# Attention with a filled-in feed-forward: half of a split filling product moved behind the third pair of scores

## The chip, the cores and the metric

The kernel runs on one core of a Trainium2 chip. The metric is the device time of one execution in microseconds (us), given as the median of several executions. The times of single instructions come from one profiled execution.

## The reference, cut to what matters

The input x has 2048 rows of 512. It is normalised row by row and goes two ways. The one is attention with 32 heads of width 16 over all 2048 rows; the other is a dense layer with a squared ReLU (width 1792), whose result gates the attention.

```
xn = layernorm(x)
q, k, v = heads(xn @ wqkv)                      # 32 heads of 16
s = softmax(q @ k.T * 0.25) @ v @ wo            # 2048 x 2048 scores a head
h = relu(xn @ w1 + b1); g = silu(h * h @ w2 + b2)
out = x + s * g
```

## The kernel before, in words

All data is float32. Projections and scores are done with a number split in a high and a low part, so that one product becomes three (high by high, high by low, low by high).

**Stages.** A first stage normalises x and makes keys, queries and values. Then comes the main loop (line 777) of 128 turns, which does the attention and, beside it, the dense layer and at the end the output projection. A short tail follows.

**Steps and turns.** A step is four heads (qd), 512 queries (qc) and 128 keys (kb); a turn handles four steps. For each step TensorE makes the scores of four heads as two pairs: `scores(i, p)` (line 291) issues two matmuls of 64 rows by 512 columns into the two banks of one PSUM tile S. The first of a pair uses rows 0 to 63 of the array ("half 0"), the second rows 64 to 127 ("half 1"), so the two can run side by side. ScalarE then takes the exponential of the whole tile (`exps`, line 284, recorded as L286). There are two S tiles in the loop, used in turn: a pair of scores must wait until the exponential of the pair two before it has read its tile. Three of four steps of a turn go that way: the turn's first and second pair (step i + 1), the third and fourth (i + 2), and the fifth and sixth (i + 4, which belongs to the next turn's values).

**Single scores.** The fourth step (i + 3) goes another way, `aside` (line 300): a single matmul into the one bank `lin`, which VectorE copies to SBUF (L305) before the next single score may use the bank. There are four in a turn, on half 0, half 1, half 0, half 1; their exponentials read the copies.

**Filling products.** The dense layer and the output projection are cut into blocks of half-height products, 64 rows by 512 columns, that accumulate in the two banks of the tile `spare`. `lin(h)` (line 357) issues the next one for half h (recorded as L330), `lin(0, 1)` one for each half. An ordinary turn issues up to twelve for each half. A list `fill` says which block belongs to which turn. In ordinary turns one product of half 1 is divided into two of 256 columns each, `lin_part(1, 0)` and `lin_part(1, 1)` (line 363, recorded as L350), so that, with the single score of half 1 between them, half 1 has as many columns as half 0. In a few turns (`make and end`) a block begins and ends in one turn; these have no divided product and are ordered otherwise.

**Values.** At the end of a turn `values` (line 555) multiplies the exponentials of four steps by the values, with all 128 rows of the array and 32 columns at a time, into the bank `acc` (L561): 16 matmuls, each recorded twice.

**What sets the order.** The program is written with a manual schedule: each engine executes its instructions in the order in which the code issues them. A wait for another engine stands on an instruction (for a matmul, on its weight load), and what is behind it on that engine comes after it. Loads and stores for later blocks are hung in by due times (`at`, `happen`) and go through the queues of SyncE and GpSimd; VectorE also evicts `spare` and splits weights, mostly while the values are multiplied.

The part of a turn around the change, lines 787 to 808:

```
for _ in range(3):
    lin(0, 1)
lin(0)
...
    lin_part(1, 0)
    aside(i + 3, 0, 1)
    lin(0)
    lin_part(1, 1)
exps(i + 2, 0, scores(i + 2, 0))
...
    lin(0, 1)
    lin(0, 1)
exps(i + 2, 1, scores(i + 2, 1))
```

Of the kernel before, what the change touches and what calls it, by code (L numbers as in the profile page):

```python
# [46 lines left out]
@with_exitstack  # L47
def mha_ffn_kernel(ctx: ExitStack, tc: tile.TileContext, x, wqkv, wo, bx, w1, b1, w2, b2, out):
    nc = tc.nc
    x, out = x[0], out[0]  # L50
    ctx.enter_context(tc.manual_schedule())
    keep = ctx.enter_context(tc.tile_pool(name="keep", bufs=1))
    dram = ctx.enter_context(tc.tile_pool(name="dram", bufs=1, space=DRAM))

    ident = keep.tile([128, 128], FT, name="ident")
    make_identity(nc, ident)
    vt = keep.tile([128, NK, VW], FT, name="vt")
    nvalid = keep.tile([1, 1], I32, name="nvalid")
    stat = keep.tile([128, 80], FT, name="stat")

    kdram = [[dram.tile([128, 2, 1024], FT, name=f"kd{g}_{h}") for h in range(2)] for g in range(4)]
    qdram = [[dram.tile([128, 2, 512], FT, name=f"qd{g}_{c}") for c in range(NC)] for g in range(4)]
    xdram = [dram.tile([128, 2, 4, 512], FT, name=f"xd{c}") for c in range(3)]

    udram = [[dram.tile([2, 2, 16, 4, 512], FT, name=f"ud{g}_{c}") for c in range(NC)] for g in range(4)]
    zdram = [[dram.tile([4, 512], FT, name=f"zd{q}_{c}") for c in range(NC)] for q in range(NQ)]
    gdram = dram.tile([S, D], FT, name="gd")

    with tc.tile_pool(name="sb", bufs=1) as sb, tc.tile_pool(name="ps", bufs=1, space=PSUM) as ps:
        fast_path(tc, sb, ps, locals())  # L70
    general_path(tc, dram, nvalid, ident, vt, kdram, qdram, gdram, x, wo, out)


def fast_path(tc, sb, ps, env):
# [11 lines left out]
    def t(shape, dt, tag):  # L86

        cnt[0] += 1
        p = ps if tag in ("S", "lin", "acc") else sb
        if tag in BUFS:  # L90
            turn[tag] = turn.get(tag, -1) + 1
            n = turn[tag] % BUFS[tag]
            tag = f"{tag}{places[n] if tag == 'S' else n}"
        return p.tile(shape, dt, tag=tag, name=f"{tag}_{cnt[0]}")
# [189 lines left out]
    def exps(i, p, src):  # L284
        if src is not None:
            act.activation(ptile[i, p], src, AF.Exp, scale=SCALE)  # L286
# [4 lines left out]
    def scores(i, p):  # L291

        if i < len(steps):
            sc = t([128, 2, 512], FT, "S")
            place(i, p)
            for hp in range(2):
                score(i, p, hp, sc[:, hp])
            return sc

    def aside(i, p, hp):  # L300

        if hp == 0:
            place(i, p)
        score(i, p, hp, single)
        dve.tensor_copy(ptile[i, p][:, hp], single)  # L305
# [51 lines left out]
    def lin(*halves):  # L357
        if pair[0]:
            for half in halves:
                j = half ^ swapped[0]  # L360
                pair[0][j].issue(half, lin_banks[j])

    def lin_part(half, part):
        if pair[0]:
            j = half ^ swapped[0]
            pair[0][j].issue_part(half, lin_banks[j], part)

    def swap():
        if pair[0]:
            while any([pair[0][half ^ swapped[0]].issue(half, lin_banks[half ^ swapped[0]]) for half in range(2)]):  # L370
                pass
            swapped[0] ^= 1
            if not swapped[0]:
                pair[0][0].evict()
                pair[0] = None
# [21 lines left out]
    def split_piece(eng=None):  # L397
        if at_piece[1] == len(pieces):
            return
        j, layer, m = pieces[at_piece[1]]  # L400
        at_piece[1] += 1
        raw, q = raws.pop(0), PAIRS[m][1]
        wf[layer, m] = [t([128, 4, 256] if layer == 1 else [128, 2, 512], FR, f"wf{layer}{p}{q}") for p in "hl"]
        split(*wf[layer, m], raw, eng or dve, pool)
        load_piece()
# [149 lines left out]
    def values(i):  # L555
        qd, qc, kb = steps[i]
        if kb == 0:
            acc[0] = t([128, 512], FT, "acc")
        for j in (1, 2, 3, 0) if i % 2 else (0, 1, 2, 3):
            o = (4 * qd + j) * 17  # L560
            mm(acc[0][32 * j:32 * j + 32], vt[:, kb, o:o + 32], ptile[i, j // 2][:, j % 2],  # L561
               start=kb == 0, stop=kb == NK - 1)

    def finish(i):

        qd, qc, kb = steps[i]
        if kb < NK - 1:
            return
        if i == len(steps) - 1:
            return  # L570
        ou = t([128, 512], FT, "ou")
        cast(act if turn_ends_first[0] else dve, ou, acc[0])
        sp.dma_start(zdram[qd][qc], ou[16::32])
        for j in range(4):
            sp.dma_start(udram[qd // 2][qc][0, qd % 2, :, j], ou[32 * j:32 * j + 16])
        n = i // 4
        events.setdefault(2 * n + 2, []).insert(0, (load_sums, (qd, qc)))
        at(n + 2, rowsums, qd, qc)
# [174 lines left out]
    def happen(time):  # L753
        for fn, a in events.pop(int(2 * time), ()):
            fn(*a)
# [10 lines left out]
    def rest(i, dst):  # L766

        group(dst, lambda p: onorm[2, 3][p][:, cut[i]], lambda p: wos[0][p][:, 3])

    def end_rest(i, src):  # L770

        o = t([128, 512], FT, f"wf2{'hl'[i // 2]}{i % 2}")
        dve.scalar_tensor_tensor(o, src, 0.5, gsb[2, i // 2][:, i % 2], op0=OP.mult, op1=OP.mult)
        pool.dma_start(out[1024 + 128 * i:1152 + 128 * i], o, accum_op=OP.add)

    turn_ends_first = [False]
    for n in range(TURNS):
        i = 4 * n
        happen(n)
        make, end, split_now = fill[n]  # L780
        if make:
            pair[0] = make()
        exps(i + 1, 0, scores(i + 1, 0))
        aside(i + 3, 0, 0)
        lin(1)
        exps(i + 1, 1, scores(i + 1, 1))
# [3 lines that stand above are left out]
        if make and end:  # L790
            lin(1)
            lin(0)
            aside(i + 3, 0, 1)
        else:

            lin_part(1, 0)
            aside(i + 3, 0, 1)
            lin(0)
            lin_part(1, 1)
        exps(i + 2, 0, scores(i + 2, 0))  # L800
        if make and end:
            for j in range(2):
                pair[0][j].issue_whole(lin_banks[j])
            swap()
        else:
            lin(0, 1)
            lin(0, 1)
        exps(i + 2, 1, scores(i + 2, 1))
        aside(i + 3, 1, 0)
        lin(1)  # L810
        exps(i + 3, 0, ptile[i + 3, 0])
        lin(0, 1)
        lin(0, 1)
        last = [scores(i + 4, 0)]
# [3 lines that stand above are left out]
        aside(i + 3, 1, 1)  # L818
        exps(i + 3, 1, ptile[i + 3, 1])
        last.append(scores(i + 4, 1))  # L820
        for p in range(2):
            exps(i + 4, p, last[p])
        if n == TURNS - 1:
            two = t([128, 2, 512], FT, "S")
            rest(0, two[:, 0])
        turn_ends_first[0] = n < LAST and end and fill[n][0] is None and fill[n - 1][2] and n % per in (7, 15, 23)
        swap()
        if n == LAST - 1:
            gsb.update({(2, i): y[2, i] for i in range(2)})
        if n == TURNS - 1:  # L830
            end_rest(0, two[:, 0])
        happen(n + 0.5)
        if split_now:
            split_piece()
        for j in range(4):
            values(i + j)
        finish(i + 3)
# [169 lines left out]
```

## Time and profile before

| | |
|---|---|
| median of 3 runs | 1267.33 us (1266.63 to 1267.73) |
| profiled execution | 1266.77 us |
| its span | 1265.00 us |
| granted TensorE clock, mean | 0.999 |
| exponentials of score tiles (L286, P<-S) | 768, mean 1020 ns |
| exponentials of copied scores (L286, P<-P) | 256, mean 1060 ns |
| copies of single scores (L305) | 512, mean 691 ns |
| value matmuls (L561), records | 4096, mean 595 ns |
| pairs of scores (L282, S), matmuls | 1536, mean 423 ns |

The span runs from the first to the last recorded instruction; the execution's own time is 1.77 us longer. PE is TensorE's matmuls, PEld its weight loads, DVE VectorE, ACT ScalarE, POOL GpSimd and SP SyncE. A row such as "S<-QA,KA 64*128 64x512" names the tile that is written and those that are read: 64 rows by 128 columns of weights, 64 by 512 of data. Matmuls are pipelined and their recorded ends are modelled: records of one half overlap, so that the time from start to start tells more than the length. "[0.21 <-ACT P L286]" behind a row is idle time of that engine ahead of it and what ended it.

### The profile page before, as it was taken

How to read it: one execution, taken by the hardware profiler on the slowest of the kernel's cores; microseconds unless marked ns; L12 is line 12 of the kernel's file. 1: busy time of each engine (PE TensorE's matmuls, PEld its weight loads, DVE VectorE, ACT ScalarE, POOL GpSimd, SP SyncE). 2: the span in 40 equal slices, each digit the busy share in tenths (PEclk: the TensorE clock that was granted, in tenths of full speed). 3: DMA queues.
4: the chain of work that ended last, by engine and by line, in shares of the span. 5: the costliest groups of instructions: out<-in, count | busy, mean ns of one | idle time of the engine just before them, and what ended most of it. 6: DMA issues, size and time to landing. Idle time of an engine off the chain costs nothing.

```text
span 1265.0 us, 24997 instructions
## 1 busy us (share of the span) xinstructions
PE 1252.7 (99%) x10029; PEld 715.2 (57%) x10029; DVE 677.8 (54%) x1064; ACT 1041.3 (82%) x1123; POOL 258.9 (20%) x150
## 2 busy tenths in 40 slices
PE   9999999999999999999999999999999999999997
PEld 7888755555555555555555555555555555545554
DVE  5542255455555654545465555555554545566655
ACT  4222588989899899999998999999889989999884
POOL 5000122122211221312023221220331212322112
PEclk9999999999999999999999999999999999999999
DMA  7565513232233132121423222333223122463445
GB/s 265 209 233 195 217 44 105 59 94 52 84 126 110 60 102 66 42 91 46 153 76 109 57 80 60 93 126 101 60 65 88 48 88 60 143 217 116 145 135 121
DMA packets 84940, 137.32 MB, mean 109 GB/s; under 512 B 26058, under 2 KB 40408, under 8 KB 83284
## 3 DMA queue, kind: packets, MB, share of 16 engines
q1 hardware_dynamic: 81668, 126.25, 30.7%
q0 software_dynamic: 2720, 8.65, 2.5%
q8 instruction: 79, 1.29, 0.4%
q10 hardware_dynamic: 432, 0.79, 0.2%
q14 instruction: 41, 0.34, 0.1%
HBM read 94.24 MB, written 41.41 MB: 107 GB/s over the span
## 4 chain that ended last, share of the span: by engine, by line
PE 96%; DVE 2%; ACT 1%; issue 1%; POOL 1%; DMA 0%; DVEq 0%; ACTq 0%
PE acc L561 36%; PE spare L330 24%; PE S L282 17%; PE S L111 9%; PE lin L282 8%; PE spare L350 1%; PE S L204 1%; ACT P L286 0%; PE spare L339 0%; POOL hl L104 0%; DMA P<-in_A_x_dram 0%; DVE P L305 0%; PE acc L111 0%; DVE st L166 0%; ACT wf2h L98 0%
## 5 line engine op out<-in xcount | busy, mean ns | idle before, releaser
L286 ACT ACTIVATE P<-S 128x1024 f32<-128x1024 f32 x768 | 739.6, 1020 | 68.1 <-PE S L282 64.9
L305 DVE COPY P<-lin 128x512 f32<-128x512 f32 x512 | 353.9, 691 | 463.0 <-PE lin L282 429.7
L561 PE MATMUL acc<-P,vt 128*32 128x512 f32 x4096 | 466.0, 595 | 0.0
L282 PE MATMUL S<-QA,KA 64*128 64x512 f32 x1536 | 344.3, 423 | 0.3
L286 ACT ACTIVATE P<-P 128x1024 f32<-128x1024 f32 x256 | 271.2, 1060 | 31.8 <-DVE P L305 31.3
L561 PEld LDWEIGHTS acc<-P,vt 128*32 128x32 f32 x4096 | 120.1, 109 | 263.8 <-issue 263.8
L282 PEld LDWEIGHTS S<-QA,KA 64*128 64x128 f32 x1536 | 163.9, 183 | 177.0 <-ACT P L286 141.1
L282 PE MATMUL lin<-QA,KA 64*128 64x512 f32 x512 | 213.8, 418 | 0.6 <-DVE P L305 0.3
L104 POOL TENSOR_TENSOR wf1l<-wr,wf1h 128x1024 fp32r<-128x1024 f32 x28 | 66.8, 2386 | 402.5 <-DVE wf1h L100 138.9
L104 POOL TENSOR_TENSOR hl<-T,hh 128x1024 fp32r<-128x1024 f32 x28 | 67.5, 2412 | 241.6 <-DVE hh L100 138.6
L330 PE MATMUL spare<-xl,wf1h 64*128 64x512 f32 x440 | 109.3, 392 | 0.0
L282 PEld LDWEIGHTS lin<-QA,KA 64*128 64x128 f32 x512 | 94.1, 184 | 26.5 <-DVE P L305 3.7
L104 POOL TENSOR_TENSOR wf2l<-wr,wf2h 128x1024 fp32r<-128x1024 f32 x28 | 66.7, 2383 | 205.6 <-PE acc L561 138.8
L330 PE MATMUL spare<-wf2l,hh 64*128 64x512 f32 x400 | 96.9, 391 | 0.0
L330 PE MATMUL spare<-xh,wf1l 64*128 64x512 f32 x504 | 96.0, 391 | 0.0
L330 PE MATMUL spare<-xh,wf1h 64*128 64x512 f32 x504 | 95.5, 390 | 0.0
L330 PE MATMUL spare<-wf2h,hh 64*128 64x512 f32 x448 | 85.6, 390 | 0.0
L330 PE MATMUL spare<-wf2h,hl 64*128 64x512 f32 x416 | 80.9, 391 | 0.0
L330 PEld LDWEIGHTS spare<-xh,wf1h 64*128 64x128 f32 x504 | 60.0, 184 | 9.8
L98 ACT CAST P<-S 128x512 fp32r<-128x512 f32 x30 | 17.6, 587 | 57.6 <-PE S L111 55.9
L330 PEld LDWEIGHTS spare<-xh,wf1l 64*128 64x128 f32 x504 | 60.0, 185 | 7.8
L330 PEld LDWEIGHTS spare<-xl,wf1h 64*128 64x128 f32 x440 | 62.4, 184 | 0.7
(210 smaller groups left out, 1107.8 us busy)
## 6 DMA issues: line engine op xcount, KB each, us to landing
wr<-in_B_w_dram SPq DMA_DIRECT2D x56, 512.0 KB
KA<-kd SPq DMA_DIRECT2D x64, 256.0 KB
QA<-qd SPq DMA_DIRECT2D x128, 128.0 KB
kd<-P SPq DMA_DIRECT2D x15, 512.0 KB
qd<-P SPq DMA_DIRECT2D x15, 512.0 KB
u<-ud SPq DMA_DIRECT2D x15, 512.0 KB
P<-in_A_x_dram SPq DMA_DIRECT2D x8, 512.0 KB
xd<-KA SPq DMA_DIRECT2D x4, 1024.0 KB
```

The source lines that it names most:

```text
L98: act.copy(dst, src)
L104: leng.tensor_tensor(lo, src, hi.bitcast(FT), op=OP.subtract)
L111: mm(dst, lhs(a, k), rhs(b, k), start=n == 0, stop=n == len(todo) - 1)
L204: nc.tensor.transpose(pt[:, k, 128 * j:128 * j + 128], xnorm[c, i][:, j, 128 * k:128 * k + 128], ident)
L282: mm(dst, k[r, p, 128 * (kb % 8):128 * (kb % 8) + 128], q[r, p], start=True, stop=True)
L286: act.activation(ptile[i, p], src, AF.Exp, scale=SCALE)
L305: dve.tensor_copy(ptile[i, p][:, hp], single)
L330: mm(bank, self.lhs(a, k)[r], self.rhs(b, k)[r], start=n == 0 and self.at[other] == 0, stop=n == len(self.todo[half]) - 1 and self.at[othe ...
L350: mm(bank[:, c], self.lhs(a, k)[r], self.rhs(b, k)[r, c], start=False, stop=False)
L561: mm(acc[0][32 * j:32 * j + 32], vt[:, kb, o:o + 32], ptile[i, j // 2][:, j % 2], start=kb == 0, stop=kb == NK - 1)
```

## The change

The second half of the divided product, `lin_part(1, 1)`, is issued behind the third pair of scores (and in the same branch as the two `lin(0, 1)` that follow) instead of in front of it. Turns with `make and end` are as before. Nothing else differs.

```
@@ -796,13 +796,13 @@
             lin_part(1, 0)
             aside(i + 3, 0, 1)
             lin(0)
-            lin_part(1, 1)
         exps(i + 2, 0, scores(i + 2, 0))
         if make and end:
             for j in range(2):
                 pair[0][j].issue_whole(lin_banks[j])
             swap()
         else:
+            lin_part(1, 1)
             lin(0, 1)
             lin(0, 1)
         exps(i + 2, 1, scores(i + 2, 1))
```

More of the change, by code (lines that the diff above doesn't have):

```diff
@@ L798, in fast_path @@
             lin(0)
-            lin_part(1, 1)
         exps(i + 2, 0, scores(i + 2, 0))
@@ L805, in fast_path @@
         else:
+            lin_part(1, 1)
             lin(0, 1)
```

## The prediction

> **What bounds the kernel now.** I read the page first, for its span, its engines and the chain that ended last, then the list of waits, then one turn of the main loop instruction by instruction.
>
> ```profile
> span 1265.0 us, 24997 instructions
> ...
> PE 1252.7 (99%) x10029; PEld 715.2 (57%) x10029; DVE 677.8 (54%) x1064; ACT 1041.3 (82%) x1123; POOL 258.9 (20%) x150
> ...
> PE 96%; DVE 2%; ACT 1%; issue 1%; POOL 1%; DMA 0%; DVEq 0%; ACTq 0%
> ```
>
> TensorE ends everything: it is 96% of the chain. ScalarE has 82%, and it shows up in the list of waits as the one engine that holds TensorE regularly, and is held by it about once a turn (108 times):
>
> ```profile
> PEld S L282 <- ACT P L286: 141.1, 277, 0.8
> ...
> ACT P L286 <- PE S L282: 64.9, 108, 0.9
> ```
>
> So the question is which of the two ends last inside a turn. I chose turn 21, because the starts in it lie close to the middle of all ordinary turns. The next lines are from the timeline of TensorE, asked in narrow windows, so that instructions that are otherwise merged stand alone (start, length, line, tile). A record of two (x2) with length 0.47 means that the second one ended 0.47 after the first began.
>
> ```profile
> 330.02 0.50 PE L282 MATMUL S<-QA,KA 64*128 64x512 f32 x2
> 330.36 0.39 PE L282 MATMUL lin<-QA,KA 64*128 64x512 f32 x1
> 330.37 0.39 PE L330 MATMUL spare<-xh,wf1h 64*128 64x512 f32 x1
> ...
> 331.64 0.46 PE L282 MATMUL lin<-QA,KA 64*128 64x512 f32 x1
> 331.75 0.39 PE L330 MATMUL spare<-xl,wf1h 64*128 64x512 f32 x1
> 331.94 0.28 PE L350 MATMUL spare<-xl,wf1h 64*128 64x256 f32 x1
> 331.98 0.39 PE L282 MATMUL S<-QA,KA 64*128 64x512 f32 x1
> 332.06 0.39 PE L282 MATMUL S<-QA,KA 64*128 64x512 f32 x1
> 332.21 0.47 PE L330 MATMUL spare<-xl,wf1h 64*128 64x512 f32 x2
> 332.67 0.45 PE L282 MATMUL S<-QA,KA 64*128 64x512 f32 x1
> ...
> 332.67 0.48 PE L282 MATMUL S<-QA,KA 64*128 64x512 f32 x2
> 332.96 0.42 PE L282 MATMUL lin<-QA,KA 64*128 64x512 f32 x1
> 332.99 0.40 PE L330 MATMUL spare<-xl,wf1h 64*128 64x512 f32 x1
> ...
> 333.45 0.40 PE L330 MATMUL spare<-xh,wf1l 64*128 64x512 f32 x2
> 333.68 0.45 PE L282 MATMUL S<-QA,KA 64*128 64x512 f32 x2
> ...
> 334.66 0.40 PE L282 MATMUL S<-QA,KA 64*128 64x512 f32 x2
> 334.99 3.64 PE L561 MATMUL acc<-P,vt 128*32 128x512 f32 x32
> 338.56 0.50 PE L282 MATMUL S<-QA,KA 64*128 64x512 f32 x2
> ```
>
> The turn is 338.56 - 330.02 = 8.54 us: 4.97 us of half-height products (scores and filling) up to 334.99, then 3.57 us of value products, which need all 128 rows and so both halves. In the first part half 0 (rows 0 to 63) and half 1 (rows 64 to 127) run side by side, each at its own pace of 0.23 us for 512 columns: half 0 from 331.75 to 331.98 to 332.21, half 1 from 332.06 to 332.29 (the x2 record ends at 332.21 + 0.47 = 332.68, less 0.39). The 256 columns of L350 take 332.06 - 331.94 = 0.12.
>
> A record longer than 0.39 is a matmul that waited for its weights after its recorded start. Here are the weight loads and the exponentials of the same turn:
>
> ```profile
> 330.02 0.18 PEld L282 LDWEIGHTS S<-QA,KA 64*128 64x128 f32 x2 [0.84 <-ACT P L286]
> 330.13 0.19 PEld L282 LDWEIGHTS lin<-QA,KA 64*128 64x128 f32 x1
> ...
> 330.37 0.19 PEld L282 LDWEIGHTS S<-QA,KA 64*128 64x128 f32 x2
> ...
> 331.61 0.18 PEld L282 LDWEIGHTS lin<-QA,KA 64*128 64x128 f32 x1
> ...
> 331.75 0.38 PEld L282 LDWEIGHTS S<-QA,KA 64*128 64x128 f32 x2
> ...
> 332.88 0.18 PEld L282 LDWEIGHTS lin<-QA,KA 64*128 64x128 f32 x1
> ...
> 333.62 0.19 PEld L282 LDWEIGHTS S<-QA,KA 64*128 64x128 f32 x2 [0.21 <-ACT P L286]
> ```
>
> ```profile
> 330.63 3.86 ACT L286 ACTIVATE P<-S 128x1024 f32<-128x1024 f32 x4 [0.60 <-PE S L282]
> ...
> 331.55 2.02 ACT L286 ACTIVATE P<-S 128x1024 f32<-128x1024 f32 x2
> ...
> 332.54 1.94 ACT L286 ACTIVATE P<-S 128x1024 f32<-128x1024 f32 x2
> ```
>
> What a load costs is in the first rows: load at 330.02, next load of the same half at 330.13, matmul record 0.50 instead of 0.39. So a matmul begins 0.11 after a load that comes late. The fifth pair of scores (333.68) thus really begins at 333.62 + 0.11 = 333.73 to 333.74, while both halves would have been free at 333.45 + 0.23 = 333.68 and 333.46 + 0.23 = 333.69. It waits because its load waits for the third exponential to give the bank back. And that exponential began at 332.54, although two exponentials can begin 0.92 apart (330.63, 331.55), that is at 331.55 + 0.92 = 332.47: it waited for the second score of the third pair, which ended at 332.06 + 0.39 = 332.45, and began 0.09 later.
>
> **The change part by part.** No instruction is added or dropped. The moved one is the second L350 of each ordinary turn:
>
> ```profile
> L350 PE MATMUL spare<-xl,wf1h x128: 270/277/284, 151.2 to 1206.9; 64*128 64x256 f32 x128
> ...
> L350 PE MATMUL spare<-wf2l,hh x96: 271/277/284, 220.5 to 1103.6; 64*128 64x256 f32 x96
> ...
> L350 PE MATMUL spare<-xl,wf2h x16: 271/276/278, 1146.2 to 1241.4; 64*128 64x256 f32 x16
> ```
>
> 128 + 96 + 16 = 240, two a turn, so 120 of 128 turns change. The order of VectorE, GpSimd, SyncE and their DMAs stays, and ScalarE's too. L350 has no wait of its own; it now stands behind the third pair's wait for the first exponential, and behind it stand four filling products and the fourth pair. That wait is over early: an exponential lasts 1.03 (the x2 record ends at 331.55 + 2.02 = 333.57, the third began at 332.54) and its bank is back 0.05 later (load at 333.62). The first exponential's bank is thus back at 330.63 + 1.03 + 0.05 = 331.71, and the load went out at 331.75, when the product of 331.75 began on that half. The cover is 0.04 us; beyond it each 0.01 us late would cost all behind it 0.01.
>
> _Loss on half 1._ The third pair's first score begins on half 0 at 331.98 as now. Half 1 is free at 331.94, where L350 starts today. Of every pair in these rows the second member starts with or after the first, and I take it that it cannot start earlier: half 1 idles 0.04. Then: second score 331.98, L350 332.21, first filling product 332.33 instead of 332.29. Half 1 is 0.04 late. Of the fourth pair (332.67) only half 0 waits for its load (0.45); half 1 goes on at its pace, 332.76 (332.67 + 0.48 - 0.39) and 332.99, so it has no slack and stays 0.04 late: 332.80, 333.03, 333.26, 333.50, free at 333.73. The single score at 332.96 is on half 0 and hangs on the copy below, which does not move, so it does not come late:
>
> ```profile
> 332.14 0.69 DVE L305 COPY P<-lin 128x512 f32<-128x512 f32 x1 [0.59 <-PE lin L282]
> ```
>
> (332.14 + 0.69 + 0.05 = 332.88, its load.)
>
> _Gain on ScalarE._ The third pair ends at 331.98 + 0.39 = 332.37 instead of 332.45; the third exponential begins at 332.46 or, by its pace, 332.47 instead of 332.54, and gives the bank back 0.07 earlier: load at 333.55, weights there at 333.66.
>
> _Sum._ Half 0 begins the fifth pair at 333.68 instead of 333.73, half 1 at 333.73 instead of 333.74. Behind it nothing waits: half 1 goes on at its pace to 334.66, and the value products need both halves. So half 0's 0.05 us is lost again and the turn changes by 0 to -0.01 us. Were ScalarE's gain nil, half 1 would still start at 333.74 as now. I take -0.005 us: 120 x -0.005 = -0.6 us. The profiled execution took 1266.77 us (span 1265.00 and 1.77 around it), so 1266.2; the median of the runs, 1267.33, stands 0.56 above it, so **1266.7 us**. The price of a shifted half is bounded by the rows: half 1 keeps 0.23 while shifted by 0.08 (332.06, 332.29), as in step; the stretch run out of step grows by some five products, and at the 0.01 us to which the rows can be read, half of it unseen in each, it could be +0.025 us a turn, +3 us in all.
>
> The rule that speaks against the change: the Trainium skill, "TensorE: Matmul & The Clock Gate", section "The mechanism" of its third part, says that matmuls start and end strictly in program order, even on different row groups. No row here shows a free half held back by the order alone, so the trace neither confirms nor denies it; by that rule half 1 loses the 0.04 us, without it the result is the faster rival below.
>
> **The rivals.** _Faster: the order does not hold the second score back._ It starts at 331.94, half 1 loses nothing, and both halves can begin the fifth pair at 333.69 instead of 333.74: about -0.04 to -0.05 us, 120 x -0.045 = -5.4 us, 1261.9. For it: each half keeps its own pace in the rows. Against it: in none of these rows does a later matmul overtake an earlier one.
>
> _Slower: the second score's weights come late._ Today its load starts at 331.75 + 0.38 - 0.18 = 331.95, when L350 begins on half 1; behind the single score it must start while that one streams on the same half (from 331.64 + 0.07 = 331.71 to 331.94). If it started only when half 1 is free, at 331.94, the score would begin 0.11 later, at 332.05: half 1 is 0.11 late instead of 0.04, free at 333.80 instead of 333.73, the fifth pair 0.06 later than now: 120 x 0.06 = +7.2 us, 1274.5. It decides from a load later than 331.98 - 0.11 = 331.87; a part of it gives a part of the price. Against it: the loads at 330.37 begin with the matmuls of 330.36 and 330.37 on the same two halves, so loads do go out under a running matmul of their own half. For it: the balance on half 1 leaves no more than 0.01 us, so any late start there is paid in full. The same page of the Trainium skill says that a load overlaps running matmuls only where the row group differs, which is this rival; the rows at 330.37 speak against the rule.
>
> That the change does not do what it says is out: the new order on TensorE shows the swap in 120 turns.
>
> **How the numbers follow.** A measurement of this kernel can tell about 0.2% (2.5 us, 0.021 us a turn) from no change. My forecast, within that: 0.60. Faster rival 0.15, slower rival 0.18, and 0.07 for a shift that costs more than the rows can show (up to +3 us and somewhat over). This gives faster 0.15, same 0.60, slower 0.25. The range reaches 4.7 us down, nearly to the faster rival, and 5.3 us up, over the cost of the shift and most of a partly late load: 1262.0 to 1272.0.
>
> **What would show it.** In an ordinary turn: the third pair as one record of 0.39 to 0.40, L350 0.23 behind it; the third exponential 2.44 to 2.45 after the turn's first score (now 2.52); of the fifth pair one member nearly without a wait (0.39 to 0.40 instead of 0.45); the value products still 4.97 after the turn's start. Wrong if the third pair's second member starts more than 0.01 us away from the first, if the fifth pair begins later than 3.71 to 3.72 after the turn's start, or if the value products move by more than 0.02 us.

## The result, and the profile after

The changed kernel takes 1262.37 us (median of 6 runs, 1262.05 to 1262.95), the kernel before in the same session 1267.46 us. The ratio is 0.996, with a 95% interval of 0.9947 to 0.9973: faster by 5.1 us, 0.4%. The forecast was no change beyond 0.2% (1266.7 us). The time lies in the range, but only 0.4 us above its lower end, and almost on the faster rival's 1261.9 us. All times here are of undisturbed executions; one of the six of experiment 2 ran at a granted clock of 0.767 and took 1516.91 us, and the time given there is the median of the other five.

The page of the changed kernel, its span, engines and chain of work:

```profile
span 1260.7 us, 24997 instructions
...
PE 1247.7 (99%) x10029; PEld 721.5 (57%) x10029; DVE 677.8 (54%) x1064; ACT 1034.2 (82%) x1123; POOL 259.0 (21%) x150
...
PE 97%; DVE 1%; POOL 1%; issue 0%; DMA 0%; ACT 0%; DVEq 0%; ACTq 0%
```

The span is 4.3 us shorter, and TensorE's busy time 5.0 us, with the same 10029 matmuls. Busy time counts overlapping records once, and a record includes a matmul's wait for its weights; so it can shrink without any matmul becoming faster. The paces are the same: 0.23 us for 512 columns of a half, and 3.57 us for the value products of a turn. ScalarE's share of the chain went from 1% to 0%, which by itself says little: in experiments 1 and 2, as fast as this kernel, it is 1%. The list of waits says more, from the side of the weight loads:

```profile
PEld S L282 <- ACT P L286: 121.6, 198, 0.8
...
ACT P L286 <- PE S L282: 64.5, 107, 0.9
```

A weight load of the scores waited for ScalarE 277 times before and 198 times now. The time in it went from 141.1 to 121.6 us; that is more than the kernel gained, since idle time of the weight loads is not all on the path.

Turn 29 of the changed kernel, again from the timeline of TensorE in narrow windows (start, length, line, tile); the turn starts at 397.26:

```profile
398.88 0.46 PE L282 MATMUL lin<-QA,KA 64*128 64x512 f32 x1
398.98 0.40 PE L330 MATMUL spare<-xl,wf1h 64*128 64x512 f32 x1
399.18 0.39 PE L282 MATMUL S<-QA,KA 64*128 64x512 f32 x1
...
399.18 0.43 PE L282 MATMUL S<-QA,KA 64*128 64x512 f32 x2
399.41 0.28 PE L350 MATMUL spare<-xl,wf1h 64*128 64x256 f32 x1
...
399.46 0.39 PE L330 MATMUL spare<-xl,wf1h 64*128 64x512 f32 x1
399.53 0.63 PE L330 MATMUL spare<-xl,wf1h 64*128 64x512 f32 x3
...
400.93 0.40 PE L282 MATMUL S<-QA,KA 64*128 64x512 f32 x2
...
402.18 3.64 PE L561 MATMUL acc<-P,vt 128*32 128x512 f32 x32
405.75 0.50 PE L282 MATMUL S<-QA,KA 64*128 64x512 f32 x2
```

Read it by the pace of 0.23 us a half. The third pair begins at 399.18 and 399.22 (the x2 record ends at 399.61, less 0.39). L350, which is on half 1 and stands behind the pair's second score, begins at 399.41: 0.23 behind 399.18, not behind 399.22. The next filling product of half 0 begins at 399.46, 0.24 behind 399.22. So the record at 399.18 is the second score, on half 1, and the one at 399.22 the first, on half 0: **the score that is issued second starts first**, as soon as its half is free. The records also carry the semaphore that, of the two, only the second score raises; by it, the second one starts first in 115 of the 118 ordinary turns between the first and the last (median 0.04 us ahead), and in none of these turns of the kernel before. (In the 8 turns without a divided product nothing was moved.) On half 1, 399.53 is 2.27 after the turn's start, as 332.29 was before: half 1 has lost nothing.

The fifth pair now has records of 0.39 to 0.40: it waits for no weights. It begins 400.93 - 397.26 = 3.67 after the turn's start (3.71 to 3.72 before: 333.73 to 333.74, less 330.02), the value products 4.92 (4.97 before), and the turn takes 8.49 us (8.54). Here is what released it, the loads and ScalarE in the same turn:

```profile
398.84 0.18 PEld L282 LDWEIGHTS lin<-QA,KA 64*128 64x128 f32 x1
398.84 0.18 PEld L330 LDWEIGHTS spare<-xl,wf1h 64*128 64x128 f32 x1
398.95 0.22 PEld L282 LDWEIGHTS S<-QA,KA 64*128 64x128 f32 x2
...
400.79 0.19 PEld L282 LDWEIGHTS S<-QA,KA 64*128 64x128 f32 x2
```

```profile
397.86 3.80 ACT L286 ACTIVATE P<-S 128x1024 f32<-128x1024 f32 x4 [0.60 <-PE S L282]
...
398.78 1.96 ACT L286 ACTIVATE P<-S 128x1024 f32<-128x1024 f32 x2
```

Four exponentials in a row take 3.80 us instead of 3.86. The third ends at 398.78 + 1.96 = 400.74 and so began some 1.03 earlier, at 399.71, 2.45 after the turn's start (2.52 before). The load of the fifth pair goes out at 400.79, 0.05 behind its end, and its weights are there at 400.90 (0.11 behind the load), before the pair's start at 400.93.

### The profile page after: what moved, and what is told of

Same layout as the page of the kernel before. It is cut to its first block, busy times and chain, and to the rows that moved or that the text cites. A ratio compares the mean times of both kernels' runs of the same rounds, so it can differ in the third digit from the quotient of the medians.

```text
span 1260.7 us, 24997 instructions
## 1 busy us (share of the span) xinstructions
PE 1247.7 (99%) x10029; PEld 721.5 (57%) x10029; DVE 677.8 (54%) x1064; ACT 1034.2 (82%) x1123; POOL 259.0 (21%) x150
## 4 chain that ended last, share of the span: by engine, by line
PE 97%; DVE 1%; POOL 1%; issue 0%; DMA 0%; ACT 0%; DVEq 0%; ACTq 0%
PE acc L561 36%; PE spare L330 25%; PE S L282 16%; PE S L111 9%; PE lin L282 8%; PE spare L350 1%; PE S L204 1%; PE spare L339 0%; POOL hl L104 0%; DMA P<-in_A_x_dram 0%; PE acc L111 0%; DVE P L305 0%; DVE st L166 0%; POOL wf2l L104 0%; PE spare L687 0%
## 5 line engine op out<-in xcount | busy, mean ns | idle before, releaser
L282 PE MATMUL S<-QA,KA 64*128 64x512 f32 x1536 | 335.1, 417 | 0.1
L282 PEld LDWEIGHTS S<-QA,KA 64*128 64x128 f32 x1536 | 147.6, 184 | 160.6 <-ACT P L286 121.6
```

The costliest lines, as they stand in the source:

```text
L282: mm(dst, k[r, p, 128 * (kb % 8):128 * (kb % 8) + 128], q[r, p], start=True, stop=True)
```

## The experiments

Four accounts had to be told apart. The theory after the result: a half starts its next matmul when that half is free, even ahead of an earlier one on the other half; that makes the third exponential 0.07 us earlier, and the gain is the wait of the fifth pair that falls away. Rival 1: the hardware keeps the order of issue, and the gain has another source. Rival 2: the gain is a better filled half 1, whatever ScalarE does. Rival 3 (for the limit of the theory): the halves are independent even of each other's waits for other engines. Medians in the starts below are over the 118 turns with two L350, worked out from the records.

**1. The order of the pair turned round.**

```
-            for hp in range(2):
+            for hp in (1, 0) if i % 4 == 2 and p == 0 else (0, 1):
                 score(i, p, hp, sc[:, hp])
```

> The changed kernel, with the two scores of the third pair issued in the opposite order: half 1 first, then half 0. Theory (a half starts its next matmul when that half is free, whatever the other half does): nothing moves; half 1 starts its score 1.92 us after the turn's start and half 0 at 1.96, as in the changed kernel, and the time is 1262.4 us within 0.5. Rival 1 (the hardware keeps the order of issue, and the early record in the changed kernel is an artefact of the records; the gain has another source): issuing half 1 first would now really start it early and win the 0.04 us a turn that I had written off, about 4 us more, 1258.

Measured: 1263.09 us, ratio 0.9967 (0.9954 to 0.998); the changed kernel's 0.996 lies in that interval, and the two cannot be told apart. The median starts of the third pair are 1.92 and 1.96 in both kernels, of L350 2.15, of the value products 4.92. Issuing half 1 first wins nothing, because it already starts first. Rival 1's 1258 us is out. (The time is 0.7 us above the forecast 1262.4, outside the 0.5 allowed.)

**2. A shorter third exponential in the kernel before.**

```
+            c = slice(0, 464 if i > 4 and i % 4 == 2 and p == 0 else 512)
-            act.activation(ptile[i, p], src, AF.Exp, scale=SCALE)
+            act.activation(ptile[i, p][:, :, c], src[:, :, c], AF.Exp, scale=SCALE)
```

The value products of steps with i % 4 == 2 that read this exponential are cut to the same columns.

> The kernel before (L350 in front of the third pair), with the third exponential of each turn cut from 1024 to 928 columns, so that it ends about 0.08 us earlier; 96 columns of one exponential and the value products of those columns are left out. Theory (the gain of the change is that the bank of the third pair comes back 0.08 us earlier and the fifth pair no longer waits for it): the same gain without moving L350. Fifth pair at 3.66 to 3.67 after the turn's start instead of 3.71, value products at 4.92, time 1262.5 to 1263. Rival 2 (the gain is that half 1 is filled better by the new order, whatever the exponential does): no gain, 1267.4.

Measured: 1262.61 us, ratio 0.9962 (0.9949 to 0.9975). L350 is where it was, and yet the whole gain is there. Turn 34 of this kernel, from the timelines of TensorE and of its loads (the turn starts at 440.33; line numbers are shifted by one or two):

```profile
444.00 0.40 PE L282 MATMUL S<-QA,KA 64*128 64x512 f32 x2
...
445.26 0.64 PE L563 MATMUL acc<-P,vt 128*32 128x512 f32 x4
...
448.83 0.50 PE L282 MATMUL S<-QA,KA 64*128 64x512 f32 x2
```

```profile
443.85 0.19 PEld L282 LDWEIGHTS S<-QA,KA 64*128 64x128 f32 x2
```

The load goes out 3.52 after the turn's start, the fifth pair begins at 3.67 without a wait, the value products at 4.93. The shorter value products are not the source of the gain: from the first of them to the next turn it is still 3.57 us (445.26 to 448.83), as in both kernels. So the earlier bank by itself gives what the change gave. Rival 2's 1267.4 is out.

**3. The same in the changed kernel**, with the same two edits.

> The changed kernel with the same third exponential of 928 columns (the same part left out). Theory: the fifth pair no longer waits in the changed kernel, so a still earlier bank gives nothing more: 1262.4 us within 0.7. Rival 2 (two separate sources that add up): a second gain of 4 to 5 us, about 1258.

Measured: 1261.93 us, ratio 0.996 (0.9947 to 0.9972). No second gain: the changed kernel and the shorter exponential remove one and the same wait.

**4. How far a score can overtake.** One more product of half 0 in front of the third pair:

```
             lin(0)
+            lin(0)
         exps(i + 2, 0, scores(i + 2, 0))
...
             lin_part(1, 1)
-            lin(0, 1)
+            lin(1)
             lin(0, 1)
```

> The changed kernel with one more filling product of half 0 issued in front of the third pair (and one fewer behind it), so that half 0 is busy until about 2.19 us after the turn's start while half 1 is free at 1.92 as before. Theory: half 1's score, issued second, starts at 1.92 and overtakes the first by 0.27 us; L350 follows at 2.15. The third pair is complete 0.23 later, the third exponential starts at 2.68, the fifth pair waits for it until about 3.9: some 0.23 to 0.25 us a turn slower than the changed kernel, about 1288 us. Rival 1 (order of issue holds): both scores start at 2.19, half 1 loses 0.27 us, L350 at 2.42, and half 1 reaches the fifth pair at 3.94: about the same time in the end, 1289 to 1292, but with both records of the third pair at 2.19.

Measured: 1285.16 us, ratio 1.0139 (1.0125 to 1.0154), 3 us below the theory's forecast and 4 us below the range of rival 1. The cost is a median of 0.21 us a turn, not 0.23 to 0.25. The time does not decide between the two; the starts do. Turn 16 of this kernel (start at 289.35), matmuls and then loads:

```profile
291.08 0.39 PE L330 MATMUL spare<-wf2l,hh 64*128 64x512 f32 x1
291.27 0.39 PE L282 MATMUL S<-QA,KA 64*128 64x512 f32 x1
...
291.31 0.39 PE L330 MATMUL spare<-wf2l,hh 64*128 64x512 f32 x1
291.50 0.28 PE L350 MATMUL spare<-wf2l,hh 64*128 64x256 f32 x1
291.55 0.39 PE L282 MATMUL S<-QA,KA 64*128 64x512 f32 x1
```

```profile
291.06 0.18 PEld L282 LDWEIGHTS S<-QA,KA 64*128 64x128 f32 x1
291.08 0.18 PEld L330 LDWEIGHTS spare<-wf2l,hh 64*128 64x128 f32 x1
291.27 0.18 PEld L350 LDWEIGHTS spare<-wf2l,hh 64*128 64x128 f32 x1
291.31 0.18 PEld L282 LDWEIGHTS S<-QA,KA 64*128 64x128 f32 x1
```

The order of issue is product (291.31), score of half 0 (291.55), score of half 1 (291.27), L350 (291.50). Both matmuls of half 1 start before the score of half 0 that was issued in front of them, by 0.28 and 0.05 us, and their loads go out before its load (291.06 and 291.27 against 291.31). The score of half 1 also starts 0.04 us before the product at 291.31, so it passes two. In all 118 turns it is the second score that starts first, by 0.27 us in the median, and L350 starts 2.15 us after the turn's start as in the changed kernel. That is no artefact of close records: matmuls of half 1, and their loads, pass those of half 0.

The semaphore shows a limit. Only the second score of a pair raises the one that releases the exponential. In the kernel before, this signal comes 0.014 us after the recorded end of the second score (medians over the 118 turns). Here it comes 0.29 us after that end, which is 0.023 us after the end of the first score, the one that was passed; in the changed kernel, too, it comes 0.023 us after the end of the first. So the start was early, but the signal still came behind the matmul issued in front, and the third exponential began behind the end of both scores in all 118 turns.

**5. L350 one pair of products further back.**

```
-            lin_part(1, 1)
             lin(0, 1)
+            lin_part(1, 1)
             lin(0, 1)
```

> The changed kernel, with L350 moved one pair of filling products further back (behind the first of the two pairs that stand between the third and the fourth pair of scores). Theory: what counts is only that nothing but the single score stands in front of half 1's score of the third pair; half 1 has the same work up to the fourth pair in any order, so its start there stays 2.73 and the time is that of the changed kernel, 1262.4 us within 0.7. Rival 2 (the filling of the gap right behind the third pair is what pays): part of the gain goes, 1264 to 1267.

Measured: 1261.82 us, ratio 0.9957 (0.9944 to 0.9971), not to be told from the changed kernel. L350 starts at 2.38 instead of 2.15, the fourth pair where it did (2.65 and 2.73). What counts is that it no longer stands in front of half 1's score of the third pair, and not which of these two places it took.

**6. L350 between the scores of the fourth pair**, behind a load that waits for ScalarE.

```
-            lin_part(1, 1)
             lin(0, 1)
             lin(0, 1)
...
                 score(i, p, hp, sc[:, hp])
+                if between and hp == 0:
+                    between()
```

Here `between` is `lin_part(1, 1)` for the fourth pair of ordinary turns.

> The changed kernel, with L350 issued between the two scores of the fourth pair, behind the half 0 score whose weight load waits for the second exponential. Half 1 is free at 2.62 us after the turn's start, that load goes out at 2.59 to 2.60. Theory, with the limit that the single score's wait shows (a load that waits for another engine holds all loads behind it, those of the other half too): L350 begins at 2.70 instead of 2.62, half 1 loses 0.08 us a turn and has nothing to win it back, value products at 5.00, about 1271 us. Rival 3 (halves are independent even of the other half's waits): L350 at 2.62, no loss, 1262.4.

Measured: 1270.98 us, ratio 1.003 (1.0018 to 1.0042), slower than before and as the theory had it; the value products begin at 5.00 (median). Turn 46 (start at 545.42; L350 is L352 here):

```profile
548.01 0.18 PEld L282 LDWEIGHTS S<-QA,KA 64*128 64x128 f32 x1 [0.22 <-ACT P L286]
548.02 0.18 PEld L352 LDWEIGHTS spare<-wf2l,hh 64*128 64x128 f32 x1
```

```profile
548.04 0.35 PE L352 MATMUL spare<-wf2l,hh 64*128 64x256 f32 x1
```

The load of half 0's score waits for the second exponential until 548.01, and the load of L352, on the other half and with no wait of its own, goes out only together with it: within about 0.01 us of it in all 118 turns, where in the changed kernel L350's load goes out 0.23 us ahead of its matmul (medians). Its record is 0.35 long instead of 0.28: half 1 was free at 548.04 and stood still for 0.07 us. Rival 3 is out: in experiment 4 a busy half 0 did not hold half 1, while here a wait of half 0 that is not yet fulfilled holds the load of half 1 behind it.

**7. An attempt at more: the divided product cut at 384.**

```
-            r, c = slice(64 * half, 64 * half + 64), slice(256 * part, 256 * part + 256)
+            r, c = slice(64 * half, 64 * half + 64), (slice(0, 384), slice(384, 512))[part]
```

> The changed kernel, with the divided product cut at column 384 instead of 256. In the changed kernel half 1 has one wait left, that of the single score behind the first L350 for VectorE's copy: free at 1.62, begins at 1.69. 384 columns take 0.05 more and fit in that wait; the 128 left take 0.11 (the time of a weight load) instead of 0.12. Theory (half 1 is now the later half by 0.01): value products 0.005 to 0.01 earlier, 1261.4 to 1262.0. Rival: half 0 or VectorE binds as well, 1262.4; or the short piece costs more than a load, and the time is above 1263.

Measured: 1262.11 us, ratio 0.996 (0.9946 to 0.9974). Inconclusive as a time. In the starts, half 1's score of the fourth pair comes 0.007 us earlier (median 2.727 against 2.734), as worked out, but the value products stay at 4.920: the small gain of half 1 does not reach the end, which fits the rival that half 0 binds as well. No variant was measurably faster than the changed kernel.

## Why the prediction was right or wrong, point by point

- **What bounds the kernel**: right. The fifth pair waited for the third exponential; taking that wait away is worth about 5 us, with or without the move (experiments 2 and 3).
- **Gain on ScalarE**: right. Third exponential forecast at 2.44 to 2.45 after the turn's start, found at 2.45 in turn 29 (median 2.46); load of the fifth pair forecast 0.07 earlier, found at 3.53 instead of 3.60.
- **Loss on half 1**: wrong, and this is the step that failed. I wrote that the second member of a pair "cannot start earlier" than the first, and charged half 1 with 0.04 us. The rows shown of turn 21 had no overtaking, but, as I noted myself, no free half held back by the order either; an absence of evidence was made a term of the sum. The whole trace of before did hold the evidence: in its second pair of scores, the one that raises the semaphore starts first in 27 of the 118 ordinary turns, by 0.005 us in the median of these and 0.016 at most. One turn was too few to rest an assumption on. Measured after the change: half 1 does not idle, its score begins at 1.92, L350 0.23 behind, and half 1 comes to the fifth pair at 3.67 instead of the forecast 3.71 (333.73 - 330.02).
- **Sum**: wrong by this term alone. Without the 0.04 us, both halves begin the fifth pair some 0.05 us earlier. In the profiled executions the 118 ordinary turns are together 5.0 us shorter, a mean of 0.042 us a turn, which matches the 5.1 us measured. My sum ended at -0.005 us a turn only because a loss of 0.04 stood against a gain of 0.05.
- **The Trainium skill** on strict program order across row groups ("TensorE: Matmul & The Clock Gate", section "The mechanism"): the runs here do not agree with it for the starts; in experiment 4 a matmul starts 0.27 us (median) ahead of an earlier one on the other half. The measurement decides. Whether the ends keep the order cannot be read from the records, whose ends are modelled; the completion signal does keep it (experiment 4). The sentence ahead of the prediction that each engine executes in the order of issue is, for the two halves of TensorE, too strong in the same way.
- **Slower rival, late weights**: it did not come true. Both loads of the third pair go out from 398.95 on, while the single score, which began at 398.88 + 0.07 = 398.95, still streams on half 1.
- **A cost of the shift**: none. Half 1 keeps 0.23 from the third pair to the fifth while it is out of step with half 0.
- **The cover of 0.04 us** for the third pair's own wait was nearly used up. It was reckoned for the load of half 0. In the changed kernel half 1's load goes out first, 0.06 us behind the end of the first exponential (median), and loads that really wait, those of the fifth pair, follow 0.05 behind: under 0.01 us is left. Experiment 6 shows what such a wait costs where it has no cover: 0.07 to 0.08 us a turn, 8.6 us in all against the changed kernel.
- **Chances and range**: no change, with a chance of 0.60, did not come true. The faster rival had 0.15; its time, 1261.9 us, was 0.5 us from the measured one. It was worked out from the same rows as the forecast and differed in one assumption. That the time fell in the range is luck: the range ended at 1262.0, just short of the mechanism that acted. Two of the stated signs of being wrong appeared: the second score starts 0.04 us away from the first (limit 0.01), and the value products moved by 0.05 us (limit 0.02).

## What to carry to other kernels

When two halves of the array run side by side, draw up a time line for each half by itself, and let a matmul start when its half is free. In these runs the order across halves bound the starts only where a wait for another engine stood; there it held the other half's next load too. So put short work of one half behind the score that another engine is waiting for, but not behind a load that will wait. Where the whole sum hangs on one assumption, look for it in all turns of the trace and not in one; and if no row can show it, both outcomes belong near the middle of the forecast.

## What the runs showed of the hardware that was not expected

- Matmuls on rows 64 to 127 pass earlier ones on rows 0 to 63, and their weight loads do so too: by 0.04 us in the changed kernel, by 0.27 us in experiment 4 (medians). No case here shows whether rows 0 to 63 pass rows 64 to 127 in the same way.
- The completion signal does not pass: in experiment 4 it comes 0.29 us after the recorded end of the score that raises it, and 0.023 us after the end of the score that was passed.
- The passing does not reach beyond a load that waits for another engine: in experiment 6 a load of the other half with no wait of its own stood behind it until 548.02 and cost half 1 0.07 us. The same can be read in the changed kernel at 398.84, where the load of a product on half 0 goes out together with the load of the single score that waits for VectorE. How many instructions can be passed was not tried; two is the most seen.
